# Evicting a PSUM bank behind both of its tiles, narrower waits for reused buffers, and another order of the last unit's products

## The chip, the cores and the metric

The kernel runs on one core of a Trainium2 chip. The metric is the device time of the program in microseconds. A core has a matrix engine (TensorE, PE in the profile, with its weight loads as PEld), VectorE (DVE), ScalarE (ACT), GpSimd (POOL), a queue engine for transfers (SyncE, SP) and 16 DMA engines. Matrix products land in PSUM, eight banks of 512 float32 columns on each of 128 partitions, and VectorE or ScalarE carries them from there to SBUF.

## The reference

Attention over 2 batches and 8 heads of 1152 rows and width 64, where each pair of neighbouring queries is averaged first, and behind it a mixture of four experts in which every expert is applied to every row.

```python
q_pool = q.reshape(B, H, S // 2, 2, D).mean(axis=3)
attn = softmax(q_pool @ k.T / sqrt(D))            # 16 heads, 576 x 1152 each
x = (attn @ v), heads side by side                # 1152 rows x 512
p = domain_probs / (domain_probs.sum(-1, keepdims=True) + 1e-09)
for e in range(4):
    h = np.maximum(x @ w1[e], 0.0)                # 512 -> 1024
    out += p[:, e:e + 1] * (h @ w2[e])            # 1024 -> 512
```

## The kernel before

**Two stages.** The attention stage runs to about 236 us, the expert stage from there to the end. In the expert stage every float32 operand is a pair of a high and a low part, and a product is made of three matmuls (high by high, high by low, low by high).

**Units.** The hidden layer is worked off in 16 units (4 experts, 4 slices each, `NU = E * 4`). Unit u has a first half, x by w1, done by seven Strassen products of half the size (`mprod`, matmuls at line 138, 12 matmuls of 288 columns each, in the PSUM chains X, Y and Z of two banks each), and a second half, h by w2, done by seven products P1 to P7 (`pprod`, matmuls at line 820) and one product L for the left-over row block (`lprod`, line 830, six matmuls of 512 columns). The loop over u interleaves by hand the second half of unit u with the first half of unit v = u + 1: P1, a Strassen product, P6, a Strassen product and so on. The order in which the code issues work is the order in each engine's queue.

**A second product.** `pprod` makes four output tiles of 128 x 256, three matmuls each, in a chain of two banks: tiles 0 and 1 share the first bank, 2 and 3 the second. The sums of Strassen's scheme accumulate in the chain: P1, P6, P7 and P4 add up in CO (banks 6 and 7), P5 and P3 likewise. After each tile `gated` (line 799, line 797 where the accumulator is first written) adds the tile times the expert's gate to the accumulator `acc` on VectorE. A bank is only ever accessed by one engine at a time, so a matmul into a bank waits until all reads of that bank that were issued before it are done, also where they read its other half; an eviction waits likewise for matmuls issued before it.

**Around it.** VectorE also adds the Strassen results (`add_part`, line 772) and makes the differences S2 and S3 (`c11_less`, line 785) and the low part of A11 (line 782). ScalarE makes ReLUs (line 775), high parts of the hidden operands (line 713), of A11 (line 778) and of weights (lines 745, 763), and evicts two products (lines 872, 915). GpSimd makes low parts (line 716), sums (788, 791), differences of weights (97, 758), and issues DMAs that add into SBUF (719, 750, 768). SyncE loads weights (90, 124). In the last unit `store` (line 812) sends each accumulator tile out, half by SyncE's and half by ScalarE's queue.

**Buffers.** The attention stage's tiles (pool `ap`: values, scores `sx`, transposed probabilities `aT` of a lower and an upper group, and small ones) are freed before the expert stage's pool `mp` (line 686) is laid over the same bytes: `acc0`, `w2s`, `w2t`, `hs`, `acc1`. The first instruction on a tile of the new pool waits until all work on the old pool is done. In the expert stage ScalarE begins with `w2_hi(0, "W")` and GpSimd with `w2_sums`, both into that pool. The first Strassen product on chain Y is evicted by ScalarE (y7, line 872), behind these splits in its queue.

Of the kernel before, what the change touches and what calls it, by code (L numbers as in the profile page):

```python
# [17 lines left out]
def attention_moe_kernel(ctx, tc, q, k, v, probs, w1, w2, out):  # L18
    nc = tc.nc
# [25 lines left out]
    NU = E * 4  # L45
# [105 lines left out]
    with ExitStack() as actx:  # L151
# [436 lines left out]
        for g in range(NTL):  # L588
            n, i = divmod(g, 9)
# [93 lines left out]
        PV_part(NP - 1, 1, 6, KT)  # L683
        actx.close()

        mp = ctx.enter_context(tc.tile_pool(name="mp", bufs=1))
        acc = [mp.tile([P, NQT, 256], F32, name="acc0")]
        w2s = mp.tile([P, 2, 10, 256], F32R, name="w2s")
        w2o = kk[1][:, 3584:].rearrange("p (z o f) -> p z o f", z=2, o=2)
# [1 line left out]
        hs = mp.tile([P, 2, 61, HALF], F32R, name="hs")  # L691
# [5 lines left out]
        CY, CZ, CX, CO = (banks[:, 2 * i:2 * i + 2] for i in range(4))  # L697

        def hop(op, z):
            if op == "L":  # L700
                return hs[:, z, 9:29:19, :]
            o, n = HS[op]
            return hs[:, z, o:o + n, :].rearrange("p k x -> p (k x)")

        def raw_of(op):
            if op == "L":
                return xr[:, 1].rearrange("p (a x) -> p a x", a=2)[:, :, 512:]
            if op == "S1A12":
                return xr[:, 3]
            return UT["C" + op[1:] if op[0] == "A" else op][:, :HS[op][1] * HALF]  # L710

        def h_hi(op, z=0):
            nc.scalar.activation(hop(op, z), raw_of(op), AF.Copy, scale=-1.0 if z else 1.0)  # L713

        def h_lo(op):
            nc.gpsimd.tensor_tensor(hop(op, 1), raw_of(op), hop(op, 0).bitcast(F32), ALU.subtract)  # L716

        def h_add(op):
            nc.gpsimd.dma_start(hop(op, 1).bitcast(F32), raw_of(op), accum_op=ALU.add)

        def rows(t):
            return t.rearrange("p o f -> p (o f)")

        def wop(u, w, z, n=1):
            if w[0] == "T":
                t, o = w2s, WT[w]
            elif w[1] == "2" and u % 2:
                t, o = w2o, int(w[2] == "2")
            else:
                t, o = w2s, 4 * (u % 2) + 2 * int(w[1] == "2") + int(w[2] == "2")  # L730
            return rows(t[:, z, o:o + n])
# [39 lines left out]
        def add_part(name, chain, part):  # L771
            nc.vector.tensor_tensor(UV[name], chain[:, :, :CW], UV[part], ALU.add)  # L772

        def relu(name):
            nc.scalar.activation(UT[name], UT[name], AF.Relu)  # L775
# [14 lines left out]
        def sum_s4():  # L790
            nc.gpsimd.tensor_tensor(UT["S4"][:, :512], UT["C12"][:, :512], UT["S2"][:, :512], ALU.add)

        def gated(u, idx, d, src):
            e, ac = u // 4, acc[d][:, idx]
            if u == 0 and (idx, d) not in seen:
                seen.add((idx, d))
                nc.vector.tensor_scalar(ac, src, pw[:, idx, e:e + 1], None, ALU.mult)  # L797
            else:
                nc.vector.scalar_tensor_tensor(ac, src, pw[:, idx, e:e + 1], ac, ALU.mult, ALU.add)  # L799
# [8 lines left out]
        def store(idx, d):  # L808
            for a in range(2):
                b, t = (a, 8) if idx == 8 else (idx // 4, 2 * (idx % 4) + a)  # L810
                eng = nc.scalar if a else nc.sync
                eng.dma_start(ov[b, t][:, d * 256:(d + 1) * 256], acc[d][a * HALF:(a + 1) * HALF, idx])

        def pprod(u, name, chain=CO):
            op, w, b, d, first = PR2[name]
            o = HS[op][0]
            for i in range(4):
                pc = chain[:, i // 2, (i % 2) * 256:(i % 2) * 256 + 256]
                for m, (x, y) in enumerate(TERMS):
                    nc.tensor.matmul(pc, hs[:, x, o + 2 * i:o + 2 * i + 2, :].rearrange("p k x -> p (k x)"), wop(u, w, y),  # L820
                                     start=(first == 1 and m == 0 and i % 2 == 0), stop=(m == 2), skip_group_check=True)
                gated(u, 4 * b + i, d, pc)
                if u == NU - 1 and name in ("P4", "P5", "P3", "P2"):
                    store(4 * b + i, d)

        def lprod(u, pc):
            for sl in range(2):
                for m, (x, y) in enumerate(TERMS):
                    c = 27 if sl else 8
                    nc.tensor.matmul(pc, hs[:, x, c:c + 2, :].rearrange("p k x -> p (k x)"), wop(u, f"W{sl + 1}1", y, 2),  # L830
                                     start=(sl + m == 0), stop=(sl + m == 3), skip_group_check=True)
            for d in range(2):
                gated(u, 8, d, pc[:, d * 256:(d + 1) * 256])
                if u == NU - 1:
                    store(8, d)
# [10 lines left out]
        def tail(u):  # L846
            add_part("C12", CZ, "u1")
            relu("C12")
            if u == NU - 1:
                h_hi("A12")  # L850
                sum_s4()
                h_lo("A22")
                h_lo("A12")
                h_hi("S4")
                h_lo("S4")
            else:
                sum_s4()
                h_hi("S1A12")
                h_hi("S1A12", 1)
                h_add("S1A12")  # L860
# [44 lines left out]
        h_lo("L")  # L905
        mprod(0, 6)
        tail(0)

    for u in range(NU - 1):
        v, w = u + 1, u + 2  # L910
        pprod(u, "P1")
        if u == 0:
            mprod(v, 1)
# [3 lines left out]
        h_lo("A22")  # L917
        h_lo("S4")
        pprod(u, "P6")
        w1_split(w, 0, 3)  # L920
        if u:
# [7 lines left out]
        if u == 0:  # L929
            mprod(v, 3)  # L930
            add_part("u2", CY, "m1")
        pprod(u, "P7")
        if u:
            mprod(v, 3)
# [35 lines left out]
        pprod(u, "P2")  # L970
        mprod(v, 6)
        tail(v)

    u = NU - 1
    for name in ("P1", "P6", "P7", "P4"):
        pprod(u, name)
    pprod(u, "P5", CZ)
    pprod(u, "P3", CZ)
    lprod(u, CY[:, 0])
    pprod(u, "P2", CX)  # L980


_INS = ['q', 'k', 'v', 'moe_domain_probs', 'moe_w1', 'moe_w2']
# [25 lines left out]
```

## Time and profile before

| | us |
|---|---|
| median of 3 runs | 943.27 |
| lowest and highest | 937.57, 945.43 |
| profiled execution | 946.92 |
| its span, first to last instruction | 945.1 |
| PE busy, PEld busy | 737.9, 624.0 |
| DVE, ACT, POOL busy | 491.7, 407.8, 411.6 |
| mean granted clock of TensorE | 0.871 |

Times in rows are microseconds from the span's start, unless marked ns. A row of a timeline has the start, the time that it took, the engine, the line, the operation, `out<-in`, shapes and the number of instructions merged in it; in brackets stands how long the engine had been idle before it and what ended that. "<-DVE acc L799" says that an instruction of line 799 on VectorE, which writes `acc`, ended the wait. The time of a merged row runs from the first start to the last end; matmuls and weight loads overlap their successors, so the distance between starts tells their rate. The granted clock is given as a share of 2.4 GHz; it has two levels, 1.0 and 0.5, and a value between them is a mean over a stretch. The DMA share is the mean busy share of the 16 DMA engines.

### The profile page before, as it was taken

The numbers are of one execution on the slowest core, as the hardware profiler recorded it, in microseconds if no ns is written. First come the engines' busy times: TensorE is split into PE (matmuls) and PEld (weight loads), VectorE is DVE, ScalarE is ACT, GpSimd is POOL, SyncE is SP. The second block draws the span as 40 slices with busy tenths as digits, with TensorE's granted clock in tenths as the row PEclk, the third lists the DMA queues.
The fourth block names the chain that finished last, engine by engine and source line by source line (L and its number), as shares of the span: only waits on it lengthen the run. The fifth ranks groups of instructions, "written<-read, shape, count | busy, mean of one in ns | idle before, by whom it ended". The sixth has DMA issues, their size and how long they took to land.

```text
span 945.1 us, 14470 instructions
## 1 busy us (share of the span) xinstructions
PE 737.9 (78%) x5609; PEld 624.0 (66%) x5609; DVE 491.7 (52%) x939; ACT 407.8 (43%) x606; POOL 411.6 (44%) x524
## 2 busy tenths in 40 slices
PE   8999999999776766767677777677776777776776
PEld 6777777776666665656666666666665766666664
DVE  6787778776544445444443434444445344444543
ACT  5676777675534342334433232334242324243210
POOL 5454555467634352524433333444262525243330
PEclk9999999999778989989985868797889789797965
DMA  5856655530552625425351525261524425152203
GB/s 158 215 147 171 170 126 141 146 99 24 128 110 44 131 43 111 88 66 111 68 118 36 112 43 115 39 128 26 128 48 106 82 71 109 45 108 45 47 2 100
DMA packets 52566, 89.91 MB, mean 95 GB/s; under 512 B 4625, under 2 KB 30481, under 8 KB 52497
## 3 DMA queue, kind: packets, MB, share of 16 engines
q0 software_dynamic: 9936, 38.87, 22.0%
q1 hardware_dynamic: 41120, 48.94, 19.5%
q10 hardware_dynamic: 1440, 1.18, 0.5%
q8 instruction: 44, 0.72, 0.3%
q14 instruction: 26, 0.20, 0.1%
HBM read 30.97 MB, written 2.36 MB: 35 GB/s over the span
## 4 chain that ended last, share of the span: by engine, by line
PE 69%; DVE 23%; issue 5%; ACT 2%; POOL 0%; DMA 0%; DVEq 0%; SPq 0%; ACTq 0%; POOLq 0%
PE banks L138 24%; PE banks L820 20%; DVE acc L799 14%; PE banks L417 8%; PE banks L214 6%; PE banks L371 6%; DVE xr L772 4%; PE banks L830 3%; PE banks L353 2%; DVE xr L785 2%; ACT hs L778 1%; DVE hs L782 1%; DVE acc L797 1%; DMA kq<-in_k_dram 0%; DVE sx L382 0%
## 5 line engine op out<-in xcount | busy, mean ns | idle before, releaser
L820 PE MATMUL banks<-w2s,hs 128*128 128x256 f32 x1152 | 231.4, 330 | 155.9 <-DVE acc L799 148.7
L799 DVE SCALAR_TENSOR_TENSOR acc<-banks,pw,acc 128x256 f32<-128x256 f32 x462 | 212.1, 480 | 216.4 <-PE banks L820 205.9
L820 PEld LDWEIGHTS banks<-w2s,hs 128*128 128x128 f32 x1152 | 183.0, 218 | 199.8 <-DVE acc L799 189.4
L775 ACT ACTIVATE xr<-xr 128x576 f32<-128x576 f32 x48 | 32.8, 684 | 284.0 <-DVE xr L772 284.0
L716 POOL TENSOR_TENSOR hs<-xr,hs 128x512 fp32r<-128x512 f32 (+2 forms) x82 | 94.8, 1173 | 86.6 <-ACT hs L713 86.2
L772 DVE TENSOR_TENSOR xr<-banks,xr 128x576 f32<-128x576 f32 x79 | 59.8, 757 | 121.4 <-PE banks L138 113.8
L382 DVE TENSOR_SCALAR_CACHE_REDUCE sx<-banks 128x1152 f32<-128x1152 f32 x72 | 97.7, 1357 | 42.4 <-PE banks L371 18.9
L138 PE MATMUL banks<-xb,kk 128*128 128x288 f32 x480 | 98.3, 353 | 4.1 <-ACT xr L872 2.8
L388 ACT ACTIVATE sx<-sx,mn 128x1152 f32<-128x1152 f32 x72 | 90.5, 1258 | 19.9 <-DVE sx L382 19.7
L750 POOL DMA_DIRECT2D w2s<-w2t x15 | 12.9, 862 | 187.2 <-ACT w2s L745 175.9
L138 PE MATMUL banks<-q2all,kk 128*128 128x288 f32 x448 | 94.4, 351 | 0.0
L138 PEld LDWEIGHTS banks<-xb,kk 128*128 128x128 f32 x480 | 87.2, 242 | 5.3 <-ACT xr L872 3.1
L713 ACT ACTIVATE hs<-xr 128x512 fp32r<-128x512 f32 (+3 forms) x112 | 78.0, 722 | 19.2 <-DVE xr L785 15.4
L417 PE MATMUL banks<-aT,vn 128*64 128x320 f32 (+1 forms) x576 | 85.5, 418 | 0.0
L138 PEld LDWEIGHTS banks<-q2all,kk 128*128 128x128 f32 x448 | 84.9, 244 | 0.0
L820 PE MATMUL banks<-kk,hs 128*128 128x256 f32 x192 | 41.3, 347 | 37.9 <-DVE acc L799 37.9
L138 PE MATMUL banks<-xa,kk 128*128 128x288 f32 x384 | 70.3, 344 | 0.0
L138 PEld LDWEIGHTS banks<-xa,kk 128*128 128x128 f32 x384 | 65.7, 233 | 0.5 <-issue 0.4
L371 PE MATMUL banks<-kk,q2all 64*128 64x512 f32 (+1 forms) x504 | 63.1, 365 | 0.5 <-DVE sx L382 0.5
L404 ACT ACTIVATE aT<-banks 128x640 f32<-128x640 f32 x72 | 50.5, 702 | 29.8 <-PE banks L214 29.6
L820 PEld LDWEIGHTS banks<-kk,hs 128*128 128x128 f32 x192 | 32.8, 234 | 45.3 <-DVE acc L799 45.1
L371 PEld LDWEIGHTS banks<-kk,q2all 64*128 64x128 f32 x504 | 54.5, 186 | 12.0 <-DVE sx L382 6.1
(126 smaller groups left out, 945.7 us busy)
## 6 DMA issues: line engine op xcount, KB each, us to landing
kk<-kq POOLq DMA_DIRECT2D x15, 896.0 KB, 8.2
hs<-xr POOLq DMA_DIRECT2D x15, 576.0 KB, 4.9
kq<-in_moe_w_dram SPq DMA_DIRECT2D x64, 128.0 KB, 2.4
qsf<-in_moe_w_dram SPq DMA_DIRECT2D x16, 512.0 KB, 7.2
w2s<-w2t POOLq DMA_DIRECT2D x15, 512.0 KB, 4.5
q2all<-q2all SPq DMA_DIRECT2D x28, 256.0 KB, 4.1
vn<-in_v_dram SPq DMA_DIRECT2D x8, 576.0 KB, 6.5
kk<-kk SPq DMA_DIRECT2D x14, 320.0 KB, 4.6
```

The lines of the kernel that those rows point to most:

```text
L138: nc.tensor.matmul(chain[:, c, :CW], w1s[u % 2][:, a, WI[wo], kt, :], xop(xo, z, kt)[:, c * CW:(c + 1) * CW], start=(first and kt == 0 and ...
L214: nc.tensor.transpose(pt[:, a, j, :], src[r], ident[r, r])
L371: mm = nc.tensor.matmul(sp[:, cs[c]], q2[n % 2][r, zq, h, ts_], src[n % 2][r, zk, cs[c]], start=(zq + zk == 0), stop=(zq == 1), skip_group ...
L382: nc.vector.tensor_scalar(sx[g % 3].rearrange("p (c x) -> p c x", c=3), spt.pop(g), -INV, None, ALU.mult, ALU.min, accum_out=mn[g % 3])
L388: nc.scalar.activation(sx[g % 3], sx[g % 3], AF.Exp, bias=mn[g % 3], scale=-1.0, accum_out=sums[n % 2][:, i:i + 1])
L404: nc.scalar.activation(dst, pt, AF.Copy)
L417: nc.tensor.matmul(po[h * HALF:(h + 1) * HALF, :w], vn[n % 2][:, h, kt, :], aT[grp][:, h, kt, :], start=(kt == 0), stop=(kt == KT - 1))
L713: nc.scalar.activation(hop(op, z), raw_of(op), AF.Copy, scale=-1.0 if z else 1.0)
L716: nc.gpsimd.tensor_tensor(hop(op, 1), raw_of(op), hop(op, 0).bitcast(F32), ALU.subtract)
L772: nc.vector.tensor_tensor(UV[name], chain[:, :, :CW], UV[part], ALU.add)
L799: nc.vector.scalar_tensor_tensor(ac, src, pw[:, idx, e:e + 1], ac, ALU.mult, ALU.add)
L820: nc.tensor.matmul(pc, hs[:, x, o + 2 * i:o + 2 * i + 2, :].rearrange("p k x -> p (k x)"), wop(u, w, y), start=(first == 1 and m == 0 and ...
```

## The change

Three edits. In `pprod` the evictions move: both tiles of a bank are computed, then both are evicted, so a product issues six matmuls, two evictions, six matmuls, two evictions instead of four times three matmuls and one eviction. The pool `mp` is declared with waits by tile: the first instruction on one of its tiles waits only for work on the old tiles whose bytes it takes over. The last unit's order becomes P1, P5, P6, P3, P7, L, P4, P2, with P1, P6, P7, P4 in chain CO, P5 and P3 in CZ, L in CY and P2 in CX; the stores follow the product that completes a tile (P7 in place of P5), and in `tail` of the last unit the low parts are made in the order S4, A12, A22 in place of A22, A12, S4.

```diff
-        mp = ctx.enter_context(tc.tile_pool(name="mp", bufs=1))
+        mp = ctx.enter_context(tc.tile_pool(name="mp", bufs=1, reuse_waits="tile"))
...
         def pprod(u, name, chain=CO):
             op, w, b, d, first = PR2[name]
             o = HS[op][0]
+            pc = [chain[:, i // 2, (i % 2) * 256:(i % 2) * 256 + 256] for i in range(4)]
             for i in range(4):
-                pc = chain[:, i // 2, (i % 2) * 256:(i % 2) * 256 + 256]
                 for m, (x, y) in enumerate(TERMS):
-                    nc.tensor.matmul(pc, hs[:, x, o + 2 * i:o + 2 * i + 2, :].rearrange("p k x -> p (k x)"), wop(u, w, y),
+                    nc.tensor.matmul(pc[i], hs[:, x, o + 2 * i:o + 2 * i + 2, :].rearrange("p k x -> p (k x)"), wop(u, w, y),
                                      start=(first == 1 and m == 0 and i % 2 == 0), stop=(m == 2), skip_group_check=True)
-                gated(u, 4 * b + i, d, pc)
-                if u == NU - 1 and name in ("P4", "P5", "P3", "P2"):
-                    store(4 * b + i, d)
+                for t in range(i - 1, i + 1) if i % 2 else ():
+                    gated(u, 4 * b + t, d, pc[t])
+                    if u == NU - 1 and name in ("P4", "P7", "P3", "P2"):
+                        store(4 * b + t, d)
...
             if u == NU - 1:
                 h_hi("A12")
                 sum_s4()
-                h_lo("A22")
-                h_lo("A12")
                 h_hi("S4")
                 h_lo("S4")
+                h_lo("A12")
+                h_lo("A22")
...
     u = NU - 1
-    for name in ("P1", "P6", "P7", "P4"):
-        pprod(u, name)
-    pprod(u, "P5", CZ)
-    pprod(u, "P3", CZ)
-    lprod(u, CY[:, 0])
-    pprod(u, "P2", CX)
+    for name, chain in (("P1", CO), ("P5", CZ), ("P6", CO), ("P3", CZ), ("P7", CO), ("L", CY), ("P4", CO), ("P2", CX)):
+        if name == "L":
+            lprod(u, chain[:, 0])
+        else:
+            pprod(u, name, chain)
```

## Rows read from the trace of the kernel before

**Rows 1.** The page's costliest groups: busy, mean ns | idle before, and its releaser.
```profile
L820 PE MATMUL banks<-w2s,hs 128*128 128x256 f32 x1152 | 231.4, 330 | 155.9 <-DVE acc L799 148.7
...
L799 DVE SCALAR_TENSOR_TENSOR acc<-banks,pw,acc 128x256 f32<-128x256 f32 x462 | 212.1, 480 | 216.4 <-PE banks L820 205.9
...
L820 PE MATMUL banks<-kk,hs 128*128 128x256 f32 x192 | 41.3, 347 | 37.9 <-DVE acc L799 37.9
```

**Rows 2.** Table by stretches: length, busy of PE, PEld, DVE, ACT, POOL, clock, DMA.
```profile
384.50:425.50 41.00, 28.51 (x176) 25.30 (x175) 19.20 (x38) 15.68 (x23) 17.22 (x19) 0.92 0.42 88
...
416.20:422.00 5.80, 5.17 (x21) 4.88 (x22) 1.45 (x3) 0.00 (x0) 1.93 (x3) 0.50 0.00 0
...
909.00:945.10 36.10, 23.78 (x87) 19.36 (x87) 14.16 (x31) 2.00 (x3) 5.11 (x4) 0.55 0.26 66
```

**Rows 3.** Timeline, weight loads: begin of P1 in unit 0 and in unit 15.
```profile
248.84 0.44 PEld L820 LDWEIGHTS banks<-w2s,hs 128*128 128x128 f32 x3
...
907.78 0.78 PEld L820 LDWEIGHTS banks<-w2s,hs 128*128 128x128 f32 x3
```

**Rows 4.** Timeline (start, us, engine, line, operation, [idle before]): line 138 and product P6.
```profile
384.47 1.63 PEld L138 LDWEIGHTS banks<-xa,kk 128*128 128x128 f32 x12
...
386.05 0.43 PEld L820 LDWEIGHTS banks<-w2s,hs 128*128 128x128 f32 x3
...
387.27 0.77 PEld L820 LDWEIGHTS banks<-w2s,hs 128*128 128x128 f32 x6 [0.79 <-DVE acc L799]
...
388.86 0.42 PEld L820 LDWEIGHTS banks<-w2s,hs 128*128 128x128 f32 x3 [0.82 <-DVE acc L799]
...
389.21 0.84 PEld L138 LDWEIGHTS banks<-xb,kk 128*128 128x128 f32 x6
```

**Rows 5.** Timeline, VectorE: two evictions of P6 in a row.
```profile
387.93 0.88 DVE L799 SCALAR_TENSOR_TENSOR acc<-banks,pw,acc 128x256 f32<-128x256 f32 x2 [0.71 <-PE banks L820]
```

**Rows 6.** Timeline, weight loads of the L product.
```profile
799.79 1.25 PEld L830 LDWEIGHTS banks<-w2s,hs 128*128 128x128 f32 x6
```

**Rows 7.** Timeline: P2 and the sums of line 785, same unit.
```profile
412.62 0.44 PEld L820 LDWEIGHTS banks<-kk,hs 128*128 128x128 f32 x3
...
413.71 1.42 DVE L785 SCALAR_TENSOR_TENSOR xr<-banks,xr 128x576 f32<-128x576 f32 x2 [1.87 <-ACT hs L778]
...
415.72 0.47 DVE L799 SCALAR_TENSOR_TENSOR acc<-banks,pw,acc 128x256 f32<-128x256 f32 x1
...
416.25 1.36 PEld L820 LDWEIGHTS banks<-kk,hs 128*128 128x128 f32 x6 [3.18 <-DVE acc L799]
```

**Rows 8.** Timeline of GpSimd and ScalarE over the same unit.
```profile
382.89 2.22 ACT L713 ACTIVATE hs<-xr 128x1152 fp32r<-128x1152 f32 x2
...
385.40 0.87 POOL L719 DMA_DIRECT2D hs<-xr  x1 [1.17 <-ACT hs L713]
...
395.50 0.86 POOL L768 DMA_DIRECT2D kk<-kq  x1
...
402.78 1.56 ACT L745 ACTIVATE w2s<-w2t 128x768 fp32r<-128x768 f32 x2
...
409.45 1.41 POOL L788 TENSOR_TENSOR xr<-xr 128x576 f32<-128x576 f32 x1 [1.04 <-ACT xr L775]
```

**Rows 9.** Table by stretches: the adds of first and second weights.
```profile
395.50:403.00 7.50, 5.93 (x39) 5.09 (x37) 3.55 (x7) 0.81 (x2) 0.86 (x2) 1.00 0.87 173
...
407.50:412.10 4.60, 3.10 (x23) 2.69 (x22) 2.51 (x5) 1.32 (x2) 2.26 (x2) 1.00 0.60 114
```

**Rows 10.** Timeline: entry into the expert stage.
```profile
236.85 2.01 ACT L745 ACTIVATE w2s<-qsf 128x1024 fp32r<-128x1024 f32 x2 [4.74 <-DVE xr L454]
...
241.57 1.81 PE L138 MATMUL banks<-xb,kk 128*128 128x288 f32 x6 [2.84 <-ACT xr L872]
```

**Rows 11.** Last eviction (timeline) and stores of line 812 (the line's own view).
```profile
941.13 0.48 DVE L799 SCALAR_TENSOR_TENSOR acc<-banks,pw,acc 128x256 f32<-128x256 f32 x1 [0.72 <-PE banks L820]
...
L812 ACTq DMA_DIRECT2D out_dram<-acc x18: 497/553/783, 922.8 to 941.7; - x18
```

## The prediction

> **What bounds the kernel now.** I read the page's costliest groups first. The expert stage's second products (line 820) let TensorE stand idle for 155.9 + 37.9 = 193.8 us, almost all of it ended by the evictions of line 799, and these in turn idle 216.4 us, ended by line 820 [rows 1]: two engines that wait for each other, neither of them full. Then the table by stretches: a whole unit (41.0 us) holds 19.20 us of VectorE, 15.68 of ScalarE and 17.22 of GpSimd, at a DMA share of 0.42 and a granted clock of 0.92; elsewhere the clock stands at 0.50, that is 1.2 GHz instead of 2.4, and the last stretch runs at 0.55 [rows 2]. So no engine fills the stage. There are sixteen units; the first product P1 of unit 0 begins at 248.84 and that of unit 15 at 907.78, so 15 periods take 658.9 us, 43.9 each, and the last unit the remaining 37.3 [rows 3].
>
> The timeline shows where they wait. Product P6 issues three matmuls at 386.05, stands 0.79 us in front of the next six, 0.82 in front of the last three, and ends where 389.21 begins: 3.16 us for 12 matmuls. Yet unhindered ones follow each other every 0.117 us (388.86 to 389.21, three) [rows 4]. The second tile of a bank waits until the first one is evicted, and so for matmul drain, a semaphore and 0.44 us of VectorE in a pair [rows 5], 0.48 alone [rows 1].
>
> **The change, part by part.** (1) Evictions after both tiles of a bank. Two waits per product go. What the new unit costs on TensorE, at the full clock: seven products of 12 x 0.118 = 1.42; seven Strassen products of line 138, 12 matmuls from 384.47 to 386.05 = 1.58 [rows 4]; one L product, six wide matmuls, 1.3 [rows 6]. Sum 9.9 + 11.1 + 1.3 = 22.3 us.
>
> What hides the moved evictions: four take 4 x 0.44 = 1.76 us [rows 5], and the product or the Strassen product that TensorE does on other banks next takes 1.58. A product's first two evictions start while its second bank fills (0.71 us), the last two end about 1.4 us behind its last matmul, so bank and chain are free before their next use. With the Strassen addition behind them (0.76) VectorE needs 2.5 us per pair of products where TensorE needs 3.0; over the unit 19.2 of 22.3 [rows 2]. If that cover went, each pair would cost up to 0.9 us, the length of two evictions.
>
> One wait stays and moves. In P2, the first eviction stands behind the sums that need the second Strassen product: this one ends at 412.62, the sums begin at 413.71, the first eviction at 415.72, and TensorE starts again at 416.25, 3.18 idle [rows 7]. Afterwards P2 no longer waits there; its four tiles and the next Strassen product run on (1.42 + 1.58 = 3.0), and P1 of the next unit waits for two evictions: 415.72 + 0.88 + about 0.05 - 412.62 = 4.05 behind the same end. What is late next is thus P1, by 4.05 - 3.0 = 1.05. Period by TensorE: 22.3 + 1.05 + some 0.1 for semaphores = 23.5 us.
>
> A second loop has the same length. From the ReLU to the next one: 0.7 for it; the two splits of S1A12, 2.22; 0.3 to the accumulating DMA's issue; from there GpSimd's queue of low parts, weight differences and DMA issues, 385.40 to 395.50, 10.1; the two splits of the second weights that wait for it, 1.56 and, for a third of the size, about 0.7; a DMA issue 0.86; S1's sum 1.41 [rows 8]; the sums and the low part, 413.71 to 415.72, 2.0 [rows 7]; four evictions and an addition, 1.76 + 0.76. Sum 22.4, with six hand-overs of about 0.1, 23.0. Every second unit issues one DMA more (0.86), 23.9. This loop is invisible now because GpSimd rests; it will lie within half a microsecond of TensorE's. Mean of the longer ones: (23.5 + 23.9) / 2 = 23.7.
>
> DMA is the third. A unit's transfers fill 0.42 x 41.0 = 17.2 us of all sixteen engines [rows 2], 73% of 23.7. Tight is the add of the new second weights: P6 needs it some 11.7 us behind the issue of the first weights' add. That add with the loads beside it fills 7.5 x 0.87 = 6.5 us, the other 4.6 x 0.60 = 2.8 [rows 9]: 9.3 if they pack, no loss; one behind the other, landing to landing, 7.5 + 4.6 = 12.1, with issue and the next loads between about 13.9, 2.2 late. I take the middle, 1.1, since rows 9 show neither case. Period 24.8, bounds 23.5 and 26.5 (both ends and 0.5 for GpSimd).
>
> The clock: at 1.2 GHz the same unit would need 84 x 0.213 + 84 x 0.240 + 2.6 = 40.7 us, nearly today's period (0.213 from the six of line 820 that start at 416.25 and take 1.36 with the last one's own drain [rows 7], in a stretch at 0.50 [rows 2]; 0.240 as 288 columns to 256). So the full clock carries the gain. I take it because the stretches that fell stand behind waits of TensorE (the 3.18 of rows 7, the long row of waits in the last unit), and the new unit has one short wait in 23.7 us.
>
> (2) Waits of the expert buffers. ScalarE's first weight split stands 4.74 us, until the last attention division; because of it the eviction of y7 is late, and TensorE idles 2.84 before 241.57, so has been through since 238.73 [rows 10]. The buffers w2s and w2t overlay score and lower-group attention tiles, which are free before. ScalarE then does the splits inside its idle time, y7 leaves as soon as its product ends, and TensorE goes on at about 238.8. Bounds 0 (another entry of ScalarE's queue holds it) to 2.8; I take 2.6, since what follows shifts as a whole. P1 of unit 0 then starts at 246.2.
>
> (3) Last unit. P1, P5, P6, P3 and so on alternate between two chains, so seven products no longer wait for their own bank. TensorE needs 7 x 1.42 + 1.3 = 11.2, VectorE 30 x 0.44 + 0.8 = 14.0: VectorE binds, from about 1.6 behind P1's start (the addition before), end of the last eviction about 15. From there to the span's end 945.1 - 941.61 = 3.5 now [rows 11]: 18.5. But the stores begin only with P3 at about 7.5, and 18 of them on ScalarE's queue at 0.553 take 10, plus about 3 to the end: 20.5. The reordered low parts let P3 start at about 5.7; the other way about S4 would come last of three. I take 21 (bounds 18.5, and 27 at the low clock) against 37.3 now.
>
> **Sum.** 246.2 + 15 x 24.8 + 21 = 639.2 us of span; the profiled execution took 946.92 for a span of 945.1, so 1.8 more: 641.0. (That execution lies 0.4% above the median of 943.27; I leave that out.)
>
> Here the wait for the bank itself ends TensorE's idle time, 186.6 us of it by line 799 alone [rows 1]. A rule that speaks against this change: the Trainium skill, TensorE: Matmul & The Clock Gate, section "HAM oscillation — how this bites in real kernels", tells of a kernel in which, once its loop was put right, PSUM double-buffering gave no further gain (126.6 to 125.5 us). By this rule of the Trainium skill the sum would be an estimate of 946.9 x 0.991 = 938 us; the trace disagrees, as its wait lies at the bank.
>
> **Rivals.** (a) GpSimd, ScalarE and DMA bind rather than TensorE: the loop of 23.9 stretches because transfers collide (the 2.2 above, and as much again where the next loads hold up the first weights), 29.5 a period. 246 + 442 + 22 + 2 = 712. For it: three loops within 5%. Against it: a unit's GpSimd work is 17.22 in total.
>
> (b) The clock falls back each time P1 waits: half of each unit at 1.2 GHz, (24.8 + 40.7) / 2 = 32.8 a period; 246 + 492 + 25 + 2 = 765. All of it low: 246 + 626 + 27 + 2 = 901. For it: 0.50 behind the 3.18 wait. Against it: that wait shrinks to a third.
>
> (c) Nothing changes but part 2: something of equal length stands behind every eviction, for instance the operands, and takes the place of the wait; 946.9 - 2.6 = 944. Against it: GpSimd and ScalarE rest for more than half of the unit [rows 2]. The rule cited above from the Trainium skill is this case.
>
> (d) Slower: VectorE becomes the bound. It works in order, and a Strassen addition now stands behind four evictions instead of one; the next Strassen product on that bank waits for it. It decides for TensorE from an eviction of (3.0 - 0.76) / 4 = 0.56 us, and makes the kernel slower from about 1.2 (seven pairs of 4 x 1.2 + 0.76, and 4.6 for L and the sums, are 43.5 a unit); at 1.3 a unit takes 46.3 and the kernel 246 + 695 + 44 + 2 = 987. Against it: 462 evictions average 480 ns whatever runs beside them [rows 1].
>
> **How the numbers follow.** Forecast 0.72, with its own range of 612 (TensorE alone: 246.2 + 15 x 23.0 + 18.5 + 1.8) to 672 (26.5 a period and 27 for the last unit). (a) 0.14, (b) 0.09, (c) 0.03, (d) 0.02. For 8 in 10 the range must reach into (a): 612 to 706. A measurement can tell about 1% from no change. Faster: 0.72 + 0.14 + 0.09 = 0.95; same 0.03; slower 0.02.
>
> **What would show it.** Part 1: line 820's idle time falls from 194 to 15 to 25 us, one wait of about 1 us in P1 of each unit; evictions come in pairs; a unit takes 24 to 26.5 at a clock above 0.95 and a DMA share near 0.7. If P6 waits for a DMA, it was the transfers; if GpSimd has no rests, the second loop; a clock of 0.5 in mid-unit is (b). Part 2: the first split starts near 232. Part 3: the last stretch takes 19 to 23, with VectorE without gaps. The prediction falls if evictions get longer, or if the clock does not hold.

## The result: 632.4 us, and the profile after

The changed kernel takes 632.37 us (median of four executions, 631.30 to 634.66), the kernel before 944.35 beside it (937.57 to 945.95): a ratio of 0.671, interval 0.667 to 0.675. Forecast were 641.0 us with a range of 612 to 706. The profiled execution took 631.3 us, its span is 629.5.

First the page of the kernel after: its span and granted clock by slices, and those of the costliest groups that answer to [rows 1] (busy us, mean ns of one | idle time before, and what ended most of it).

```profile
span 629.5 us, 14474 instructions
...
PEclk9999999999999999899999999999999999999997
...
L799 DVE SCALAR_TENSOR_TENSOR acc<-banks,pw,acc 128x256 f32<-128x256 f32 x462 | 190.0, 475 | 26.5 <-PE banks L820 18.3
L820 PE MATMUL banks<-w2s,hs 128*128 128x256 f32 x1152 | 155.0, 284 | 15.0 <-DVE acc L799 13.9
L820 PEld LDWEIGHTS banks<-w2s,hs 128*128 128x128 f32 x1152 | 147.0, 191 | 19.9 <-ACT hs L713 17.0
...
w2s<-w2t POOLq DMA_DIRECT2D x15, 512.0 KB, 8.4
```

The matmuls of line 820 idle 15.0 us instead of 155.9, the evictions 26.5 instead of 216.4 [rows 1]. One eviction takes 475 ns (480 before). The second weights' add now lands 8.4 us behind its issue.

Next a table by stretches of the same kernel: length, busy time of PE, PEld, DVE, ACT, POOL, granted clock, DMA share. The first row is the middle of the expert stage, the second 24 us inside it, the third the last unit. They answer to [rows 2].

```profile
250.00:600.00 350.00, 334.38 (x2527) 326.76 (x2526) 258.86 (x555) 228.41 (x335) 260.67 (x286) 1.00 0.71 147
...
388.00:412.00 24.00, 23.21 (x178) 22.75 (x178) 18.12 (x40) 15.91 (x25) 17.66 (x20) 1.00 0.61 127
608.00:629.50 21.50, 11.95 (x90) 11.29 (x90) 13.24 (x33) 2.01 (x3) 6.65 (x6) 0.84 0.44 111
```

TensorE is now the full engine (334 of 350 us) at a clock of 1.00, 2.4 GHz; 24 us hold the work that took 41. Then the timeline of the same kernel, weight loads of TensorE: the entry of unit 0, a stretch of one unit, and the start of unit 15 (start, us, engine, line, operation, count, [idle before and what ended it]).

```profile
238.86 0.82 PEld L138 LDWEIGHTS banks<-xb,kk 128*128 128x128 f32 x6 [0.18 <-ACT xr L873]
...
245.04 1.51 PEld L820 LDWEIGHTS banks<-w2s,hs 128*128 128x128 f32 x12
...
389.17 1.52 PEld L820 LDWEIGHTS banks<-kk,hs 128*128 128x128 f32 x12
...
393.25 1.50 PEld L820 LDWEIGHTS banks<-w2s,hs 128*128 128x128 f32 x12 [1.00 <-ACT hs L713]
...
396.25 1.52 PEld L820 LDWEIGHTS banks<-w2s,hs 128*128 128x128 f32 x12
397.70 0.84 PEld L138 LDWEIGHTS banks<-xb,kk 128*128 128x128 f32 x6
...
607.97 4.38 PEld L820 LDWEIGHTS banks<-w2s,hs 128*128 128x128 f32 x36 [1.50 <-ACT hs L713]
```

Where [rows 4] show three loads, a wait, six, a wait, three, a product is now one row of twelve: P6 at 396.25 takes 1.45 us to the next start (1.42 had been forecast). P2 (389.17) no longer waits for the 3.18 of [rows 7]; what is left is 1.00 in front of P1 (393.25). P1 begins at 245.04 in unit 0 and at 607.97 in unit 15, against 248.84 and 907.78 [rows 3]: fifteen periods take 362.9 us instead of 658.9, 24.2 each instead of 43.9, and the last unit 21.5 instead of 37.3. The 315.6 us of span are 3.8 at the entry, 296.0 in the periods and 15.8 in the last unit.

VectorE of the same kernel, timeline around that P1:

```profile
390.26 1.42 DVE L785 SCALAR_TENSOR_TENSOR xr<-banks,xr 128x576 f32<-128x576 f32 x2 [1.42 <-ACT hs L778]
...
392.26 1.65 DVE L799 SCALAR_TENSOR_TENSOR acc<-banks,pw,acc 128x256 f32<-128x256 f32 x4
```

The evictions come four in a row. P2's begin at 392.26, behind the sums of line 785; two of them are done at about 393.1, and P1 starts at 393.25. So this wait is for P2's first bank, though the row of the weight load names line 713: two releases came close together, and the page gives the matmul's own wait to line 799.

**How much was waiting, how much the clock.** Taken from all weight loads between P1 of unit 0 and P1 of unit 15: before, 211 gaps of more than 0.6 us from one start to the next sum to 278.0 us, and all other spacings to 380.9; after, 18 gaps sum to 24.1 and the others to 338.8, 0.131 each. The 193 gaps that are gone would count 25.2 us as ordinary spacings. So 278.0 - 24.1 - 25.2 = 228.7 us of the gain were waits, and 380.9 + 25.2 - 338.8 = 67.3 us came from closer spacing: 15.2 and 4.5 us a unit. The second part is the clock: in the kernel before, 690 of the ordinary spacings lie where the clock stood at 0.50 and average 0.230 us, the other 1709 average 0.130, as those after do.

### The profile page after: what moved, and what is told of

The parts are those of the page before. It is cut to its first block, busy times and chain, and to the rows that moved or that the text cites. A ratio compares the mean times of both kernels' runs of the same rounds, so it can differ in the third digit from the quotient of the medians.

```text
span 629.5 us, 14474 instructions
## 1 busy us (share of the span) xinstructions
PE 596.3 (95%) x5609; PEld 528.9 (84%) x5609; DVE 468.8 (74%) x939; ACT 406.3 (65%) x606; POOL 413.8 (66%) x524
## 5 line engine op out<-in xcount | busy, mean ns | idle before, releaser
L799 DVE SCALAR_TENSOR_TENSOR acc<-banks,pw,acc 128x256 f32<-128x256 f32 x462 | 190.0, 475 | 26.5 <-PE banks L820 18.3
L820 PE MATMUL banks<-w2s,hs 128*128 128x256 f32 x1152 | 155.0, 284 | 15.0 <-DVE acc L799 13.9
L820 PEld LDWEIGHTS banks<-w2s,hs 128*128 128x128 f32 x1152 | 147.0, 191 | 19.9 <-ACT hs L713 17.0
L772 DVE TENSOR_TENSOR xr<-banks,xr 128x576 f32<-128x576 f32 x79 | 59.6, 755 | 42.3 <-PE banks L138 31.5
L138 PE MATMUL banks<-xb,kk 128*128 128x288 f32 x480 | 77.6, 298 | 2.1 <-DVE xr L772 2.1
L763 ACT ACTIVATE kk<-kq 128x768 fp32r<-128x768 f32 (+2 forms) x57 | 51.8, 957 | 30.1 <-POOL kq L97 27.8
L138 PEld LDWEIGHTS banks<-xb,kk 128*128 128x128 f32 x480 | 67.9, 191 | 3.2 <-DVE xr L772 2.5
L138 PEld LDWEIGHTS banks<-q2all,kk 128*128 128x128 f32 x448 | 65.2, 190 | 0.0
L214 PEld LDWEIGHTS banks<-ident,sx 64*128 64x128 f32 x1296 | 54.4, 139 | 6.1 <-issue 2.7
L214 PE MATMUL banks<-ident,sx 64*128 64x64 f32 x1296 | 57.9, 225 | 1.2 <-ACT raw L237 0.5
L97 POOL TENSOR_TENSOR kq<-kq 128x256 f32<-128x256 f32 x64 | 50.0, 802 | 6.9 <-DMA kq<-in_moe_w_dram 5.7
```

Of the source, the lines that this page charges most:

```text
L138: nc.tensor.matmul(chain[:, c, :CW], w1s[u % 2][:, a, WI[wo], kt, :], xop(xo, z, kt)[:, c * CW:(c + 1) * CW], start=(first and kt == 0 and ...
L214: nc.tensor.transpose(pt[:, a, j, :], src[r], ident[r, r])
L763: nc.scalar.activation(flat(w1s[u % 2][:, z, a:b]), flat(wf[:, a:b]), AF.Copy, scale=-1.0 if z else 1.0)
L820: nc.tensor.matmul(pc[i], hs[:, x, o + 2 * i:o + 2 * i + 2, :].rearrange("p k x -> p (k x)"), wop(u, w, y), start=(first == 1 and m == 0 a ...
```

## The experiments

Two theories on the gain stood against each other at first. Theory: TensorE waited for its own banks, and part 1 alone removes that. Rival: the clock carries it, and any shortening of the waits that keeps the clock up brings most of it. Then a second question: which of three loops of nearly equal length (TensorE with P1's wait; GpSimd and ScalarE; the transfers) sets the 23.7 us.

### The parts one by one

**Part 1 alone**, in the kernel before:

```diff
+            pc = [chain[:, i // 2, (i % 2) * 256:(i % 2) * 256 + 256] for i in range(4)]
...
-                gated(u, 4 * b + i, d, pc)
+                for t in range(i - 1, i + 1) if i % 2 else ():
+                    gated(u, 4 * b + t, d, pc[t])
```

> The paired evictions alone, on the kernel before (buffer waits and the last unit's order as before). Theory: they carry nearly everything. A unit stays at 23.9 us (14 waits per unit gone), what is missing is the entry into the expert stage (P1 of unit 0 at about 248.8 instead of 245.0, 3.8 us) and in the last unit the chain CO used by four products in a row, where VectorE sets the pace anyway: 1.5 us. 632.4 + 3.8 + 1.5 = 638. Rival: the last unit's order is worth the ten or more microseconds by which that unit got shorter (37.3 to 21.5); then 648 or more.

Measured: 635.94 us (634.25 to 636.18), ratio 0.682 (0.677 to 0.688), 3.6 us above the changed kernel and near the theory's 638. Weight loads of this kernel, timeline: P1 of unit 0 and of the last unit; then a matmul row of the last unit.

```profile
248.92 1.53 PEld L820 LDWEIGHTS banks<-w2s,hs 128*128 128x128 f32 x12
...
611.56 1.49 PEld L820 LDWEIGHTS banks<-w2s,hs 128*128 128x128 f32 x12 [1.50 <-ACT hs L713]
...
613.82 1.67 PE L820 MATMUL banks<-w2s,hs 128*128 128x256 f32 x12 [0.57 <-DVE acc L799]
```

It begins unit 0 at 248.92, as before [rows 3], takes 362.6 us for fifteen periods, and 22.5 for the last unit (span 634.1), where products still wait 0.3 to 0.6 us for the evictions of the one before them in the same chain. Part 1 is the whole gain but for about 3.9 us at the entry and 1.0 at the end.

**Part 2 alone**: `reuse_waits="tile"` in the kernel before, nothing else.

> The waits by tile alone, on the kernel before. Theory: TensorE's wait of 2.84 us for y7 goes, and the additions behind it on VectorE come earlier with it: P1 of unit 0 at 245 instead of 248.8, 940.5 against 944.4. Rival: the wait of P1 in unit 0 for the sums (2.95 us there) absorbs it, and the time stays within 1 us of 944.

Measured: 936.55 us (920.14 to 949.18) beside 936.05 (925.25 to 957.11) of the kernel before on the same chip. The time can't tell; the trace can. Weight loads of this kernel, timeline:

```profile
245.02 0.45 PEld L820 LDWEIGHTS banks<-w2s,hs 128*128 128x128 f32 x3
249.59 1.35 PEld L820 LDWEIGHTS banks<-w2s,hs 128*128 128x128 f32 x6 [4.12 <-DVE acc L797]
```

P1 starts at 245.02 instead of 248.84 [rows 3], 3.8 us early, and then stands 4.12 in front of its second tile; the kernel before goes on there at 252.43, so 2.8 are left. Both kernels spread by 30 us from one execution to the next, and the time follows the mean granted clock (925.25 us at 0.909, 957.11 at 0.859, in the kernel before); a part worth 3 us does not show in that.

**Part 3 alone**: the order of the last unit, evictions tile by tile as before.

```diff
-    for name in ("P1", "P6", "P7", "P4"):
-        pprod(u, name)
...
+    for name, chain in (("P1", CO), ("P5", CZ), ("P6", CO), ("P3", CZ), ("P7", CO), ("L", CY), ("P4", CO), ("P2", CX)):
```

> The last unit's order and chains alone (with its low parts in the new order and the stores moved), each tile still evicted behind its own three matmuls. Theory: TensorE works in order, so the second tile of a bank waits inside each product as before, and alternating chains only hide the wait between products, which the kernel before does not have: last unit 35 to 37 us instead of 37.3, 942 to 944 in all. Rival (the prediction's sentence that these products no longer wait for their own bank holds by itself): last unit some 25, 932.

Measured: 943.59 us (942.33 to 957.44), ratio 1.012 (0.997 to 1.026): no gain that can be told. Weight loads of this kernel, timeline of the last unit:

```profile
913.04 0.79 PEld L820 LDWEIGHTS banks<-w2s,hs 128*128 128x128 f32 x3
914.72 0.78 PEld L820 LDWEIGHTS banks<-w2s,hs 128*128 128x128 f32 x6 [0.89 <-DVE acc L799]
916.31 0.78 PEld L820 LDWEIGHTS banks<-w2s,hs 128*128 128x128 f32 x6 [0.82 <-DVE acc L799]
```

The rows of six run across the end of a product: alternating chains takes away the wait between two products, but inside each one a wait of 0.8 in front of the second tile of either bank stays. The last unit takes 29.9 here (913.04 to 942.9) instead of 37.3, less than the theory's 35 to 37. That is the clock and not the order: with part 2 alone, which keeps the old order, the last unit takes 28.9 (889.46 to 918.36). Tables by stretches of the last unit (columns as above), part 2 alone and part 3 alone:

```profile
889.50:918.30 28.80, 15.69 (x92) 12.26 (x91) 13.88 (x31) 2.00 (x3) 5.12 (x4) 0.91 0.33 83
```

```profile
913.10:942.90 29.80, 16.92 (x92) 13.22 (x91) 14.06 (x31) 2.00 (x3) 5.15 (x4) 0.84 0.31 80
```

The clock was 0.91 and 0.84 there, and 0.55 in [rows 2]; the order brings no gain that shows.

**The changed kernel again**, on another chip, as a ruler for what follows.

> The changed kernel once more, as the yardstick for the three below on the same chip: 632, a unit of 23.7 to 23.9 us, P1 waiting 1.0 to 1.2 us in each of them.

Measured: 632.03 us (631.42 to 632.34), ratio 0.674 (0.670 to 0.679), with the same periods.

### One bank of two

The changed kernel, with the first bank's tiles evicted one by one again, so that half of the waits come back:

```diff
-                for t in range(i - 1, i + 1) if i % 2 else ():
+                for t in (i,) if i < 2 else range(2, 4) if i == 3 else ():
```

> The changed kernel, but in the first bank of every product each tile is evicted behind its own three matmuls again, the second bank stays paired: one wait per product instead of two or none. Theory (time goes with the number of waits, about 1.0 us each, and the clock holds at 1.0): a unit takes 22.3 + 7 x 1.0 + 1.0 = 30.3, in all 245 + 455 + 26 + 2 = 728. Rival (the clock decides): with a wait in every product the granted clock falls as in the kernel before, mean 0.85 or less, a unit takes 34 or more, and the time is 780 or more.

Measured: 792.15 us (791.88 to 793.54), ratio 0.851 (0.844 to 0.857). Both expectations missed: the time is above the theory's 728 and in the rival's range, and yet the clock is 0.96, above the rival's 0.85. Weight loads and evictions of this kernel, timeline around P6:

```profile
397.11 0.45 PEld L820 LDWEIGHTS banks<-w2s,hs 128*128 128x128 f32 x3
398.70 1.13 PEld L820 LDWEIGHTS banks<-w2s,hs 128*128 128x128 f32 x9 [1.15 <-DVE acc L799]
...
397.50 0.76 DVE L772 TENSOR_TENSOR xr<-banks,xr 128x576 f32<-128x576 f32 x1 [0.78 <-ACT w2s L745]
398.18 0.48 DVE L799 SCALAR_TENSOR_TENSOR acc<-banks,pw,acc 128x256 f32<-128x256 f32 x1
```

The wait in the first bank is longer than the one in the second (0.82 [rows 4]): the eviction of the first tile stands on VectorE behind the Strassen addition that began at 397.50. It starts at 398.18, when that addition lets go of the engine. The other products of this kernel wait 0.78 to 1.22 there, and P2 again 3.18.

Its units take 34.2 us, all but the first; the shortest of before take 41.1, those of after 23.7. Again from start to start, and less an ordinary spacing, seven waits of the second bank cost 7 x 0.88 = 6.2 us of the 6.9 between 41.1 and 34.2. The seven of the first bank are 0.97, 1.34, 1.35, 1.41, 1.28, 1.26 and P2's 3.37; less the spacings and less P1's new wait (1.05) that is 9.0 of the 10.5 between 34.2 and 23.7. The rest, 0.7 and 1.5, is the clock. Tables by stretches show where it is low, first of this kernel, then two of the kernel before:

```profile
384.90:388.50 3.60, 3.60 (x19) 3.60 (x20) 1.36 (x3) 0.00 (x0) 1.89 (x3) 0.62 0.00 0
...
390.00:414.00 24.00, 19.02 (x135) 17.75 (x136) 13.78 (x29) 13.82 (x20) 14.59 (x17) 1.00 0.59 118
```

```profile
384.50:416.00 31.50, 21.31 (x144) 18.81 (x142) 15.53 (x31) 13.45 (x20) 13.81 (x16) 0.99 0.55 115
...
586.20:589.40 3.20, 3.20 (x14) 3.20 (x15) 0.48 (x1) 0.72 (x2) 0.86 (x1) 0.50 0.00 0
```

In the unit shown, of either kernel, the clock falls behind P2's wait of 3.18 (here to 0.62 over 3.6 us, in the kernel before to 0.50 [rows 2]), and stands at 0.99 to 1.00 across the products with their waits of 0.8 to 1.2. In the kernel with one bank this holds for every unit but the first. In the kernel before it holds for units 1 to 3 only: from unit 4 on the clock also falls in mid-unit, as in the last row, behind waits of 1.22 and 0.82 us. Of the 205.6 us at 0.50 between P1 of unit 0 and P1 of unit 15, 80 lie between the start of a P2 and the next P1, 125 elsewhere (tails of such stretches included). The rival falls: half of the gain was missing although the clock held.

### Which loop sets 23.7 us

**P2 in another chain** takes away the wait in front of P1:

```diff
-        pprod(u, "P2")
+        pprod(u, "P2", CY)
```

> The changed kernel with product P2 of the loop in chain CY instead of CO: P1 of the next unit then finds CO free and no longer waits for P2's evictions (VectorE's order is unchanged). Theory A (TensorE with the wait at P1 sets the period): P1 waits only for A11's low part, some 0.2 us, a unit takes 22.9, in all 632 - 13 = 619. Theory B (the loop over GpSimd and ScalarE stands right behind, 23.0 and 23.9 by turns): the unit takes 23.4, 626, and the wait shows up as one for A11's low part or for S2. Theory C (transfers): the wait reappears at P6 for the DMA that adds T2, 630.

Measured: 629.18 us (628.89 to 630.48); the changed kernel on the same chip took 632.03. The waits moved. Here is the view of waits of this kernel from 268 to 600 us, rows of line 820 (us in total, times, longest), and P6 in the timeline, behind its first load:

```profile
PEld banks L820 <- DMA w2s<-w2t: 6.7, 10, 1.1
...
PEld banks L820 <- DVE hs L782: 5.0, 5, 1.6
...
275.70 1.37 PEld L820 LDWEIGHTS banks<-w2s,hs 128*128 128x128 f32 x11 [0.78 <-DMA w2s<-w2t]
```

In the kernel after, the same view has 15.5 us in 14 waits in front of P1 and 1.4 in one for that transfer. Now P6 waits for the second weights' add in ten units, P1 for A11's low part in five, and units take 22.8 to 25.5 from P1 to P1. The time and the wait at P6 are theory C's; the waits at P1 are the sign that theory B named. TensorE alone does not set the period any more; another loop is about as long.

**The low part of A11 earlier** as well, S3 in front of S2 in the same list:

```diff
-        c11_less("S2", "S1")
         c11_less("S3", "C21")
         a11_lo()
-        h_hi("S2")
+        c11_less("S2", "S1")
         h_hi("S3")
+        h_hi("S2")
```

> As the one before, and VectorE makes S3 and A11's low part before S2, which waits for GpSimd's sum S1. Theory A: the last 0.2 us go, 22.7 a unit, 616. Theory B: S2 and the loop behind it are where they were, so the time is within 3 us of the run before. Theory C: 630.

Measured: 635.97 us (632.29 to 638.23), slower than without and outside all three theories. P1 no longer waits; from unit 4 on, units alternate between 22.8 and 25 to 28, and TensorE waits 10.2 us in eight times for the second weights' add and 8.2 in six for the first weights'. What was saved in one unit is given back to the transfers in the next.

**Without the first weights' sums** on GpSimd behind unit 1, in that kernel:

```diff
-        if u >= NU:
+        if u >= NU or u > 1:
```

> As the one before, with the differences of the first weights left out from unit 2 on (four GpSimd instructions a unit, 2.9 to 3.2 us; the sums then hold old values, so this part of the computation is missing). Theory B: GpSimd's loop gets 3 us shorter and the unit falls to TensorE's 22.4, so this run is 8 us or more below the one before. Theory A: no difference beyond 2 us.

Measured: 615.74 us (614.72 to 616.62), 20 below the run before, as theory B had it. View of waits of this kernel, 268 to 600 us, and the table of that stretch (columns as above):

```profile
PEld banks L820 <- DVE xr L772: 1.3, 1, 1.3
...
PEld banks L820 <- DMA w2s<-w2t: 1.1, 2, 0.8
...
268.00:600.00 332.00, 329.11 (x2511) 322.89 (x2511) 259.25 (x556) 218.37 (x326) 217.91 (x224) 1.00 0.72 150
```

A unit takes 22.8 us, with hardly a wait: this is TensorE alone. The DMA share is 0.72, as in the kernel after, and the second weights' add still needs 8.5 us; so the transfers are not too many, they had been issued too late: this add is issued 16.7 to 17.6 us behind the unit's P1 here, 18.5 to 21.7 in the run before (units 1 to 13). Its issue stands on GpSimd, behind its sums. The second loop is GpSimd's queue and what lies behind it, ScalarE's splits of these sums included; which member of the loop counts most was not separated.

### Versions that try to use it

The second weights' sums (line 758) from GpSimd to VectorE, once in the kernel with S3 first, once with P2's chain alone, once in the changed kernel itself, and in a last one only the first two of the four sums. Edit, beside the ones above:

```diff
-                nc.gpsimd.tensor_tensor(w[o], w[x], w[y], op)
+                eng.tensor_tensor(w[o], w[x], w[y], op)
...
-        w2_sums(range(4))
-        load_w2(w)
...
             add_part("u2", CY, "m1")
+        w2_sums(range(4), nc.vector)
+        load_w2(w)
```

All four sums, with P2 in CY and S3 first:

> P2 in CY, A11's low part before S2, and the differences of the second weights made by VectorE (behind the addition u2) instead of GpSimd: 3 us a unit less on GpSimd, some 1.7 more on VectorE, everything computed. Theory (GpSimd's loop and the DMA issues behind it hold the unit at 23.7): as in the run without the first weights' differences, 22.8 to 23.0 a unit, 616 to 620. Rival (VectorE, then at 20.9 of 22.8 us, delays its evictions and TensorE waits for banks again): 630 or more.

Measured: 628.76 us (628.10 to 628.85), far from the theory's 616 to 620. All four, with P2 in CY alone:

> The same without the reordering on VectorE (S2 before A11's low part). Theory: P1 waits some 0.2 to 0.5 us for A11's low part, 23.1 a unit, 619 to 623. Rival: VectorE binds, 630 or more.

Measured: 629.55 us (628.72 to 630.50), again nearer to the rival. All four, in the changed kernel:

> The changed kernel (P2 in CO) with the differences of the second weights on VectorE, nothing else. If P1's wait for P2's evictions sets the period, as the prediction's sum has it (22.3 + 1.05 + 0.1 = 23.5), a lighter GpSimd brings little: 23.5 a unit instead of 23.7 to 23.8, and no more late transfers, 627 to 630. If GpSimd's loop sets it, the unit falls below 23.2 and the time below 624.

Measured: 630.84 us (630.80 to 631.28), a little above the expectation. T1 and T2 on VectorE, T3 and T4 on GpSimd, the rest as in the first:

> As the run with all four differences of the second weights on VectorE (628.8), but only T1 and T2 there, T3 and T4 on GpSimd again: VectorE's extra load is 1.2 us instead of 2.5, GpSimd's relief 1.5 instead of 3. If both loops bind as the runs so far say (VectorE's evictions held up the Strassen product on CZ by 0.67 us, GpSimd's chain 0.9 us too long in every second unit), both waits go and a unit takes 22.9 to 23.3: 617 to 623. If the two loads only trade places, it stays at 628 to 630.

Measured: 625.93 us (624.14 to 629.27), ratio 0.667 (0.663 to 0.671), again above the expectation.

The third of them settles a term. Its units take 23.9 with P1's wait of 1.00 in each and no late transfer: TensorE's loop with that wait is 22.8 + 1.0, and a lighter GpSimd does not shorten it. So in the changed kernel TensorE with P1's wait sets the 23.7, and the loop over GpSimd binds only when that wait is gone. In the first, VectorE is the next: it holds the sums where it should evict. VectorE and weight loads of that kernel, timeline of one unit:

```profile
400.90 0.56 DVE L758 TENSOR_TENSOR w2t<-qsf 128x256 f32<-128x256 f32 x1
401.49 0.85 DVE L758 TENSOR_TENSOR w2t<-w2t,qsf 128x256 f32<-128x256 f32 x1
402.26 0.95 DVE L758 TENSOR_TENSOR w2t<-qsf 128x256 f32<-128x256 f32 x1
403.13 0.41 DVE L758 TENSOR_TENSOR w2t<-qsf,w2t 128x256 f32<-128x256 f32 x1
...
406.62 0.82 PEld L138 LDWEIGHTS banks<-xb,kk 128*128 128x128 f32 x6 [0.67 <-DVE acc L799]
```

The Strassen product at 406.62 waits 0.67 for evictions that the sums have made late, as it does in twelve units (7.0 us); the second weights' add is late there too, 3.7 us in six waits. With two of the four sums (the last version) that is gone, but the second weights' add is late again, 9.8 us in eight waits. That version is the fastest seen that computes everything, 1.0% under the changed kernel; they ran on different chips, and the intervals of their ratios (0.663 to 0.671, 0.667 to 0.675) touch, so a gain is likely, not settled. The gain from P2's chain is small but was measured beside the changed kernel: 0.45%, with ranges that don't meet.

## Why the prediction was right, point by point

**Mechanism.** Right. The two waits per product went, the evictions stayed short (475 ns), nothing of equal length stood behind them. Part 1 alone gives 635.94, so the rival that only part 2 counts falls, and with it the cited rule of the Trainium skill on PSUM double-buffering (TensorE: Matmul & The Clock Gate, section "HAM oscillation — how this bites in real kernels"): 0.671 here, not 0.991.

**TensorE's unit.** 22.3 forecast, 22.8 in the kernel that hardly waits; P1's wait 1.05 forecast, 1.00 in the rows. Loop 23.5 forecast, 23.9 measured in the kernel with lighter GpSimd. (The terms given for P1's wait add up to 4.03 and 1.03, not 4.05 and 1.05.)

**The second loop.** Right that there is one of this length: 23.0 and 23.9 by turns were forecast, units of 23.65 and 23.8 by turns make up most of the kernel after. In the longer ones it shows in the timeline of GpSimd and VectorE:

```profile
412.27 1.77 POOL L788 TENSOR_TENSOR xr<-xr 128x576 f32<-128x576 f32 x1
...
414.07 1.42 DVE L785 SCALAR_TENSOR_TENSOR xr<-banks,xr 128x576 f32<-128x576 f32 x2 [1.58 <-POOL xr L788]
```

S1's sum ends at 414.04, and line 785 waits for it and not, as at 390.26, for ScalarE. So this loop adds some 0.15 us to every second unit, and does not set the others, as the run with a lighter GpSimd shows. The loop of forecast (a) thus exists, but at TensorE's length; it does not stretch to 29.5. (That figure does not follow from its terms either: 23.9 + 2.2 + 2.2 is 28.3.)

**The transfers.** This is the term of the sum that was mis-sized. 1.1 us a unit had been taken from a middle of 0 and 2.2; in the fifteen periods TensorE waited for the adds in one unit only, here in the timeline of its weight loads:

```profile
370.15 1.10 PEld L138 LDWEIGHTS banks<-xa,kk 128*128 128x128 f32 x8 [0.40 <-DMA kk<-kq]
...
372.74 1.38 PEld L820 LDWEIGHTS banks<-w2s,hs 128*128 128x128 f32 x11 [1.36 <-DMA w2s<-w2t]
```

That is 1.8 us over all, 0.1 a unit. The two adds overlap, and lie between the two cases that the prediction set out: the second one's landing went from 4.5 to 8.4 us, the first one's stayed near 8 (8.2 and 7.7), and the share rose to the 0.71 that had been forecast. From the issue of the first to the landing of the second it is 11.0 to 12.0 us in units 1 to 13 (13.1 in the one that waited), against 9.3 if they pack and 13.9 if they queue. P6 starts 11.2 to 12.0 us behind that issue (11.7 had been forecast; 13.8 in the unit behind the one that waited, itself longer), so a duration in the middle of the two cases costs nothing, while the prediction took the middle of the two losses. The margin is narrow: in most units the landing lies between 0.2 us behind P6's start and 1.0 ahead of it. That the loss stayed away was partly luck, and it came back as soon as units got shorter or the issue later (the runs with P2 in CY).

So 15 x 1.0 us of the forecast did not come. Some 6 of them were taken back, 4.1 by unit 0, which takes 27.8 us and which the forecast priced like the others. There a product of line 138 waits 1.91 us for an addition, and the clock stands at 0.50 behind it, from about 254 to 257 us (timeline of weight loads, kernel after):

```profile
253.76 1.26 PEld L138 LDWEIGHTS banks<-xb,kk 128*128 128x128 f32 x6 [1.91 <-DVE xr L772]
```

Two units of 24.2 and 24.5, not followed further, took most of the rest. Period 24.2 instead of 24.8: 9.1 of the 9.7 us by which the span came out below 639.2.

**The clock.** The step "so the full clock carries the gain" was wrong as a reason, though the clock did hold (0.99 over the execution, forecast above 0.95). The 40.7 at 1.2 GHz and the 43.9 of before are near each other by chance: of the 19.7 us that a unit lost, 15.2 were waits and 4.5 the clock. The page had the measure: TensorE's weight loads idle more than its matmuls, which count as busy for 330 ns each where the next may start 0.13 us later; the prediction read the matmuls alone. In the kernel before, page, same columns as [rows 1]:

```profile
L820 PEld LDWEIGHTS banks<-w2s,hs 128*128 128x128 f32 x1152 | 183.0, 218 | 199.8 <-DVE acc L799 189.4
...
L820 PEld LDWEIGHTS banks<-kk,hs 128*128 128x128 f32 x192 | 32.8, 234 | 45.3 <-DVE acc L799 45.1
```

These are 245.1 us of idle time against the 193.8 of the matmuls. The forecast did not suffer, since it built the new unit from its instructions and did not subtract waits from the old one. The experiment with one bank did suffer: it priced eight waits at 8.0 us where the rows give 10.1 beyond the ordinary spacing, 3.2 of them at P2, and put the clock at nothing where it cost 1.5 a unit.

**The entry.** 2.6 forecast within 0 to 2.8, 3.8 measured, outside the bounds. The wait before y7's eviction fell from 2.84 to 0.18, as foreseen, which brings 2.7 (238.86 instead of 241.57). The other 1.1 is the clock. Tables by stretches behind that point, in the kernel before and after:

```profile
241.57:244.79 3.22, 3.22 (x13) 3.22 (x14) 1.96 (x4) 2.33 (x5) 1.71 (x3) 0.50 1.09 210
```

```profile
238.86:241.20 2.34, 2.34 (x19) 2.34 (x18) 2.00 (x5) 2.33 (x5) 0.00 (x0) 1.00 1.13 226
```

Before, the clock stood at 0.50 behind the wait of 2.84, and the 18 loads of the next products took 3.85 us; now they take 2.38 at 1.00. The Strassen product behind them waits 0.64 for an addition instead of 0.25 and starts at 241.88 instead of 245.67. "What follows shifts as a whole" is the step that failed here: the wait had also slowed what follows, and the forecast put that at nothing. Run alone, part 2 shows the same 3.8 and then loses 1.0 in front of P1's second tile. The first split begins at 232.22, where 232 had been forecast.

**The last unit.** 21 forecast, 21.5 measured. The stores' own view in the kernel after, line 812 (duration ns min/median/max, first and last start):

```profile
L812 ACTq DMA_DIRECT2D out_dram<-acc x18: 552/556/862, 614.8 to 626.2; - x18
```

As the prediction worked out, the stores and not VectorE set the end: the last eviction is done at 621.8, the last store is issued at 626.2 and the span ends 3.3 us behind it. Forecast were a first store 7.5 us behind P1's start (6.8 measured), ten microseconds of issue (11.4 from first to last start) and three to the end. The clock of this stretch is 0.84. Part 3 was said to make seven products no longer wait for their own bank; without part 1 it does not, as the run of it alone shows. Beside part 1 it is worth about 1.0.

## What to carry to other kernels

Where an eviction follows each tile of a PSUM bank that the next tile writes as well, TensorE pays the drain, the queue in front of the eviction and the eviction itself every time (0.8 to 1.2 us of idle weight loads here); evict behind the bank's last tile, and let the next product use another bank. Build the new period from its instructions, for every engine's queue by itself, and expect the gain to stop at the second longest loop: here two lay within 1%, the transfers close behind them, and most of what one more wait was worth came back as another. The kernel before also has a spread of its own (30 us of 940, against 3 of 632 after) that goes with its granted clock; the kernel with one bank, with half of the waits, spreads by 2 of 792. So a small part of a change is read from its place in the trace, or on top of the large one.

## What was not expected of the hardware

- Not each wait brought the clock down. With seven waits a unit it fell behind the longest alone (3.18 us), in units 1 to 14; with fourteen it also fell in mid-unit behind waits of 0.8 to 1.2 us, in some units and not in others (0.99 over 31.5 us in unit 3, 0.50 at 586 us). In the kernel after it fell once in the fifteen periods, behind the wait of 1.91 in unit 0, and not behind P1's waits of 1.0 to 1.84. So taking away the longest wait of each unit might bring only a part of the 4.5 us; alone, it wasn't tried.
- An add of VectorE over two operands in SBUF took 0.41 us alone and 0.56 to 0.95 beside GpSimd's adds of line 97, whose four took 3.61 us there, against 3.25 in the kernel after, where VectorE makes no such adds. The Trainium skill, SBUF — State Buffer, section "Who interferes with whom", says that a VectorE instruction with two SBUF inputs contends with a GpSimd instruction that reads SBUF; these rows agree. The evictions, with one operand in PSUM, stayed at 475 ns.
- An accumulating transfer of 512 KB took 8.4 us to land instead of 4.5, at a share of 0.71 instead of 0.39, and made TensorE wait in one unit of fifteen.
